# The prologue of a convolution and maxout kernel: x1's load moved up, work moved between ScalarE and GpSimd, a conv product made once instead of twice

## The chip, the cores and the metric

The kernel runs on one core of a Trainium2 chip. The metric is the device time of one execution in microseconds (us). The engines are named as in the profile: PE is TensorE's matmul, PEld its weight load, DVE is VectorE, ACT is ScalarE, POOL is GpSimd, SP is the engine that issues most of the DMA transfers. A q behind a name is the engine's sequencer.

## The reference

```
w = softmax(weight, axis=-1)                 # weight [8 heads, 7 taps], 1e-9 added to the sum
y[b, s, h, :] = sum over k of w[h, k] * x[b, s - 6 + k, h, :]    # zeros ahead of each sequence
h = maximum(maximum(y @ w1, y @ w2), y @ w3)                     # [tokens, 768]
out = h @ w_out                                                  # [tokens, 192]
```

x is 8 sequences of 4160 tokens by 192 channels in float32 (8 heads of 24 channels), w1, w2 and w3 are 192 x 768, w_out is 768 x 192. The output has 33280 tokens by 192 channels.

## The kernel before, in words

The 33280 tokens are cut into 65 blocks of 512. Every instruction is placed by hand: an engine executes its instructions in the order in which the program issues them, and waits only for semaphores on data and on buffers that it reuses.

The maxout is rewritten so that one of its three products becomes part of the output: with differences `wd` = w1 - w3 and w2 - w3 the hidden values are max(relu(y(w1 - w3)), y(w2 - w3)), and y(w3 w_out) is added to the output. `make_wd(n, j0, j1)` makes the differences (L312) for column tiles j0 to j1 of 128; wd[0] and wd[1] hold the first 128 channels of the two, wd[2] the last 64 of both (one in each half of the partitions), wd[3] a copy of half of wd[0] and wd[1] in the other half of the partitions (`cross_wd`, L323). `copy_w3` (L316) doubles the last 64 rows of w3 into the upper half of the partitions, which wd[2] needs. `cast_w3` (L320) casts w3 to float16 for `transpose_w3` (L338, L341), and `make_m` (L347, L349) multiplies w3 and w_out into `m16`.

The first four blocks ("dense", 0 to 3) are convolved in another way than the rest. `load_x(t)` (L167) brings 112-row windows of x; `cast_dense` (L216) casts them into two zeroed tiles xz, in which the heads' channels are kept apart, and `conv_dense` (L388) multiplies them with the banded matrix `band` of the taps, five windows (of 103 or 100 tokens) to a block. A matmul here fills 32 output partitions, so that four stand side by side in TensorE. The 192 channels are six slots of 32. Slots 0 to 3 go to PSUM tile D0, copied to yd[:, 0]; slots 4 and 5 go twice to PSUM tile D1, into both halves of the partitions, copied to yd[:, 2] (L393):

```
slots_ = ((0, 1, 2, 3), (4, 5, 4, 5))[n]
```

`cross` (L399) copies halves of yd[:, 0] across the partitions into yd[:, 1]. The hidden products of blocks 0 and 1 are made in pairs of column tiles by `l1_dense` (L541): "F" are the products over 128 channels, "H" the third products over the last 64; blocks 2 and 3 use `l1` (L517), with three products for each of two halves. `tops` and `top` (L500, L505) make relu and maximum on ACT and DVE. `first_hidden` (L613) and `first_rest` (L621, L626) make block 0's output, `st2` (L582) the others'; L589 and L590 add two PSUM halves of the output.

PSUM tiles come from three rotating pools: psp and psq have two buffers each, psw has four. pm0 and pm1 of `make_m` take the two buffers of psp, and the first product of block 2 (lp) takes the one that pm0 had. G, the conv's PSUM tiles of the later blocks, and po, the output's, share psw.

Later blocks (from 4 on) are loaded as 39-row windows into seven tiles xf, cast by POOL (L199), convolved in groups (L367), and turned by DMA transposes (L421); POOL copies the result across the halves (`double`, L430). Rows 32 to 63 of the tiles xf must be zero: `zero_x` does that, on ACT by a copy of zeros (L140) or on a named engine by a memset (L137).

The prologue's order on SP is x0, w3, w1 and w2 (128 rows, columns 0 to 255: `load_wa`, L229), the same columns of their last 64 rows (`load_wb`, L233), x1, and then the rest of the weights, w_out, x2, x3 and x4 to x6. Until the first conv can start, PE makes dummy products (L261).

Of the kernel before, what the change touches and what calls it, by code (L numbers as in the profile page):

```python
# [19 lines left out]
GRP = 24  # L20
BAND_W = 128 + PAD
NBLK = 512
CHK = 103
HALF = P // 2
# [4 lines left out]
def kernel(  # L29
# [12 lines left out]
    nc = tc.nc  # L42
# [3 lines left out]
    H, KWs = weight.shape  # L46
# [180 lines left out]
    def load_wa(f):  # L227
        for st, n, wsrc in ((w3s, 0, moe_w3), (ws, 0, moe_w1), (ws, 1, moe_w2)):
            nc.sync.dma_start(out=st[:, n, f], in_=wsrc[0:P, f])  # L229

    def load_wb(f):
        for st, lo, n, wsrc in ((w3s, 0, 1, moe_w3), (ws, 0, 2, moe_w1), (ws, HALF, 2, moe_w2)):
            nc.sync.dma_start(out=st[lo:lo + HALF, n, f], in_=wsrc[P:D, f])  # L233
# [6 lines left out]
    wos = const.tile([P, NJ, D], FP32)  # L240
    load_x(0)
    load_wa(slice(0, PW))
    load_wb(slice(0, PW))
    load_x(1)
    load_wa(slice(PW, 2 * PW))
    load_wb(slice(PW, DFF))
    load_wa(slice(2 * PW, DFF))
# [4 lines left out]
    make_identity(nc, ident[:])  # L252
    ident16 = const.tile([P, P], FP16)
    nc.gpsimd.tensor_copy(out=ident16[:], in_=ident[:])
    idle = const.tile([P, NBLK], FP16)
    nc.vector.memset(idle[:], 0.0)
    def keep_warm(widths, pool, tag):
# [24 lines left out]
    nc.vector.reciprocal(out=wrec[:], in_=wrec[:])  # L282
    zero_x(4)
    nc.vector.tensor_scalar_mul(out=line[0:NHEAD, 31:31 + KW], in0=wexp[:, 0:KW], scalar1=wrec[:])
    for v in range(2):
        nc.vector.memset(xz[1][v][:], 0.0)
    cast_dense(0, (nc.vector.tensor_copy, nc.vector.tensor_copy))
    CUT = 28
    for lo, hi, copy in ((0, CUT, nc.scalar.copy), (CUT, WIN, nc.vector.tensor_copy)):
        bps = psq.tile([32, hi - lo + 3, NHEAD], FP32, tag="q", name=f"band_{lo}")  # L290
        for c in range(lo, hi):
# [4 lines left out]
        for a in range(4):  # L296
            copy(out=band[32 * a:32 * a + 32, :, 32 * a + lo:32 * a + hi],
                 in_=bps[:, 0:hi - lo, :].rearrange("p c h -> p h c"))
    zero_x(5)
    keep_warm((NBLK,) * 3, psp, "p")  # L300


# [11 lines left out]
    def copy_w3(copy, j0, j1):  # L314
        f = slice(P * j0, P * j1)
        copy(out=w3s[HALF:P, 1, f], in_=w3s[0:HALF, 1, f])  # L316
# [56 lines left out]
            slots[t0] = ysp.tile([P, 2, nu, 2, D], FP16, tag="ys", name=f"ys_{t}")  # L373
        convs[t0] = G, heads[0]

    def conv_dense(t, copies, pools=((None, None),) * 2, order=(0, 1)):


        yd = dense[t] = ydp.tile([P, NC, NBLK], FP16, tag="yd", name=f"yd_{t}")
        for n in order:  # L380
            slots_ = ((0, 1, 2, 3), (4, 5, 4, 5))[n]
            pool, tag = pools[n]
            ps = (pool or psw).tile([P, NBLK], FP32, tag=tag or "w", name=f"D{n}_{t}")
            for (q, b, row_lo, rlen, lo, hi, cc) in chunks_of[t]:
                for v in range(2):
                    for g, s in enumerate(slots_):
                        h = (32 * s + 31 * v) // GRP
                        nc.tensor.matmul(  # L388
                            ps[32 * g:32 * g + 32, lo:hi],
                            lhsT=xz[t][v][0:rlen, q, 32 * s:32 * s + 32],  # L390
                            rhs=band[0:rlen, h, cc:cc + hi - lo],
                            start=(v == 0), stop=(v == 1), tile_position=(0, 32 * g))
            copies[n](out=yd[:, 2 * n, :], in_=ps[:])  # L393

    def cross(t, *copies):

# [294 lines left out]
    GP = nc.gpsimd.tensor_copy  # L691
    make_wd(0, 0, 2)
    make_wd(1, 0, 2)
    zero_x(6, 4, NR, nc.vector)
    conv_dense(0, (ACT, DVE))
    zero_x(6, 0, 4)
    for t in range(NDENSE, XBUF):
        load_x(t)
    copy_w3(DVE, 0, 2)
    make_wd(2, 0, 2)  # L700
    cast_dense(1, (GP, ACT), (1, 2, 0))
    l1_dense([(0, 0, PQ), (0, 1, PQ)], "F")
    cast_w3(0, 2)
    copy_w3(GP, 2, 6)
    make_wd(2, 2, 4, nc.gpsimd)
    for n in range(NC):
        make_wd(n, 4, 6, nc.gpsimd)
    cast_w3(2, 6)
    conv_dense(1, (DVE, ACT), order=(1, 0))
    make_wd(0, 2, 4)  # L710
    make_wd(1, 2, 4)
    cross_wd(0, GP)
    GP(out=wo[:], in_=wos[:])
    l1_dense([(0, 0, PQ), (0, 1, PQ)], "H")
    tops((0, 0), (0, 1))
    l1_dense([(1, 0, WW), (1, 1, WW)], "HF")
    tops((1, 0), (1, 1))
    l1_dense([(0, 2, PQ), (0, 3, PQ)], "FH")
    tops((0, 2), (0, 3))
    l1_dense([(1, 2, WW), (1, 3, WW)], "HF")  # L720
# [5 lines left out]
    tops((1, 4), (1, 5))  # L726
    transpose_w3((PQ[0], PQ[0], PQ[1]))
    cast_dense(3, (GP, GP))
    cross_wd(1, ACT)
    first_hidden(0)  # L730
    first_hidden(1)
    conv_dense(2, (ACT, DVE), (WW[0], PQ[1]))
    cast_x(4)
    cross(2, ACT, DVE)
    make_m(0)
# [26 lines left out]
    for t in range(2, NB):  # L762
        u = convs_at.get(t, NB)
        late = t > 2 and u < NB
        if t in (3, 4):
            double(t + 1)
        if t > 3:
            for v in range(casts.get(t - 1, 8) + 1, casts[t] + 1):
                cast_x(v)
        l1(t, 0)  # L770
        if t == 2:
            first_rest()
        elif t == 3:
            cast_x(8)
            nc.gpsimd.tensor_copy(out=m16[0:HALF, 2, :], in_=m16[HALF:P, 0, :])
            nc.gpsimd.tensor_copy(out=m16[HALF:P, 2, :], in_=m16[HALF:P, 1, :])
        if t > 3 and not late:
            op(lambda t=t: (store(t - 2, 0, 4, (nc.sync,)),
                            turn(t + 2, (2,)) if place(t + 2)[1:] in ((0, 4), (0, 5)) else None,
                            turn(t + 1, (4,)) if place(t + 1)[1:] == (0, 5) else None, load_on(t)))  # L780
        else:
            op(lambda t=t: store(t - 2, 0, 4, (nc.sync,)))
        cuts = ROOM if late else EVEN
        st2(t - 1, (cuts[0], cuts[0]))
        for j in range(1, NJ):
            l1(t, j)
            if late and j == 1:
                st2(t - 1, (cuts[0] + OWN + AHEAD, cuts[0] + OWN))
                meet()
                quad, second = u >= QUADS, u < QUADS or t == u - 3  # L790
                conv(u, WPWQ, range(4 * second, 4 * second + 4) if quad else range(NHEAD))
                for i in (0, 2):
                    evac(u, i)
                for i in (1, 3):
                    evac(u, i, nc.vector.tensor_copy)
                if second:
                    turn(u)
                load_on(t)
            if t == 2 and j == 1:
                meet()  # L800
                conv_dense(3, (ACT, DVE))
                zero_x(1, NQ, NR, nc.vector)
                cross(3, GP, GP)
                load_x(8)
                cast_x(6)
            elif t == 2 and j == 3:
                meet()
                conv(u, WW)
                evac(u, 0)
# [40 lines left out]
```

## Time and profile before

| what | value |
|---|---|
| median of 3 runs | 453.1 us (452.54 to 453.47) |
| profiled execution | 452.5 us, of which the profile's span is 450.7 us |
| PE, busy share of the span | 99% |
| DVE, ACT, POOL | 79%, 71%, 45% |
| granted TensorE clock | 1.0 |
| DMA, mean | 160 GB/s |
| first matmul of a dense conv | 6.22 us |
| first output store issued | 26.74 us |

All times inside a profile are counted from the start of its span. The profiled execution lies 0.6 us below the median of the runs. A row of the timeline gives start, duration, engine, source line, operation, the tiles out<-in, the shape, how often, and in brackets the idle time before it with what ended that. A merged row's duration is that of all its instructions together.

### The profile page before, as it was taken

The page shows a single profiled execution, that of the slowest core. Times are in us where ns is not written, and L with a number is a line of the kernel's source. Part 1 is how long each engine was busy: PE and PEld are TensorE (multiplying, and loading weights), DVE is VectorE, ACT ScalarE, POOL GpSimd, SP SyncE. Part 2 cuts the span into 40 slices and gives each one's busy share as a digit, 9 for nine tenths or more (in the row PEclk, how much of TensorE's full clock was granted, in tenths as well). Part 3 has the DMA queues.
Part 4 walks back from the last instruction along what each step waited for, and adds up shares of the span by engine and source line. Part 5 has one row for each costly group of instructions (what it writes and reads, how often), then busy time and mean ns, then how long its engine had stood idle before and what let it go on. Part 6 is the DMA issues. An engine that isn't in the chain of part 4 may idle for free.

```text
span 450.7 us, 18261 instructions
## 1 busy us (share of the span) xinstructions
PE 444.7 (99%) x7576; PEld 409.5 (91%) x7576; DVE 356.5 (79%) x610; ACT 320.3 (71%) x600; POOL 204.0 (45%) x234
## 2 busy tenths in 40 slices
PE   7999999999999999999999999999999999999997
PEld 4579999999999999999999999999999999999996
DVE  7778778878778787787887887887887887887775
ACT  7977677767677676776776777776776776776664
POOL 2874836556464524714724635526544545124000
PEclk9999999999999999999999999999999999999999
DMA  7978999495977759649559749769549566172123
GB/s 204 238 191 158 208 183 240 134 217 148 183 208 161 184 107 214 172 112 205 158 138 185 190 103 193 192 105 218 157 116 207 160 157 151 48 139 75 56 71 106
DMA packets 128242, 72.01 MB, mean 160 GB/s; under 512 B 52320, under 2 KB 127967, under 8 KB 128159
## 3 DMA queue, kind: packets, MB, share of 16 engines
q1 hardware_dynamic: 127999, 70.75, 68.8%
q8 instruction: 59, 0.97, 1.0%
q14 instruction: 24, 0.20, 0.2%
q10 hardware_dynamic: 160, 0.10, 0.1%
HBM read 33.28 MB, written 25.56 MB: 131 GB/s over the span
## 4 chain that ended last, share of the span: by engine, by line
PE 97%; DMA 1%; SPq 1%; issue 0%; DVE 0%; POOL 0%; POOLq 0%
PE po L582 36%; PE lq L517 32%; PE lp L517 22%; PE G L367 3%; PE lw L541 1%; DMA xf<-in_x_dram 1%; PE D L388 1%; PE lp L541 1%; PE po L613 0%; PE po L640 0%; SPq L233 0%; SPq L229 0%; PE pm L347 0%; PE lq L541 0%; SPq L167 0%; PE pt L338 0%
## 5 line engine op out<-in xcount | busy, mean ns | idle before, releaser
L582 PE MATMUL po<-wo,h 64*128 64x192 f16 x3024 | 331.7, 243 | 0.0
L505 DVE TENSOR_TENSOR h<-r,lq 128x512 f16<-128x512 f16 x384 | 263.0, 686 | 84.3 <-ACT r L500 74.3
L500 ACT ACTIVATE r<-lp 128x512 f16<-128x512 f32 x384 | 229.0, 597 | 113.4 <-PE lp L517 103.0
L517 PE MATMUL lp<-yp,wd 64*128 64x512 f16 x1098 | 295.6, 376 | 0.0
L517 PE MATMUL lq<-yp,wd 64*128 64x512 f16 x1098 | 295.5, 376 | 0.0
L582 PEld LDWEIGHTS <-h 64*128 64x128 f16 x3024 | 242.6, 94 | 5.5 <-issue 4.1
L517 PEld LDWEIGHTS <-wd 64*128 64x128 f16 x2268 | 181.6, 94 | 14.9 <-issue 0.2
L199 POOL CAST x<-xf 103x768 f16<-103x768 f32 x122 | 97.2, 825 | 112.4 <-DMA xf<-in_x_dram 108.9
L582 PE MATMUL po<-m,yp 64*128 64x192 f16 x720 | 140.3, 243 | 0.0
L430 POOL COPY yp<-yp 64x1536 f16<-64x1536 f16 (+1 forms) x70 | 90.9, 1298 | 87.3 <-DMA yp<-ys 62.3
L590 DVE TENSOR_TENSOR o<-a,po 128x384 f32<-128x384 f32 x126 | 69.0, 548 | 0.0
L582 PEld LDWEIGHTS <-yp 64*128 64x128 f16 x720 | 66.3, 94 | 0.1
L589 ACT COPY a<-po 128x384 f32<-128x384 f32 x126 | 59.5, 472 | 0.0
L407 ACT CAST ys<-G 128x480 f16<-128x480 f32 (+1 forms) x53 | 25.4, 530 | 9.5 <-PE G L367 9.5
L407 DVE CAST ys<-G 128x480 f16<-128x480 f32 (+1 forms) x53 | 30.2, 610 | 0.0
L367 PE MATMUL G<-x,band 39*32 39x240 f16 (+3 forms) x1024 | 16.5, 242 | 0.0
L367 PEld LDWEIGHTS <-band 39*32 39x32 f16 x1024 | 10.2, 91 | 4.6 <-issue 4.1
L517 PE MATMUL lq<-yd,wd 64*128 64x512 f16 x36 | 9.7, 376 | 0.0
L517 PE MATMUL lp<-yd,wd 64*128 64x512 f16 x36 | 9.7, 376 | 0.0
L541 PEld LDWEIGHTS <-wd 128*128 128x128 f16 (+1 forms) x48 | 3.1, 96 | 6.0 <-issue 2.8
L216 POOL CAST xz<-xf 112x160 f16<-112x160 f32 (+2 forms) x15 | 4.3, 330 | 7.9 <-DMA xf<-in_x_dram 7.8
L388 PEld LDWEIGHTS <-xz 112*32 112x32 f16 x320 | 3.9, 96 | 2.7 <-POOL xz L216 1.1
(79 smaller groups left out, 98.1 us busy)
## 6 DMA issues: line engine op xcount, KB each, us to landing
xf<-in_x_dram SPq DMA_DIRECT2D x113, 234.0 KB
out_dram<-o SPq DMA_DIRECT2D x62, 384.0 KB
wall<-in_moe_w_dram SPq DMA_DIRECT2D x12, 128.0 KB
xf<-in_x_dram SPq DMA_DIRECT2D x7, 204.8 KB
xf<-in_x_dram SPq DMA_DIRECT2D x3, 420.0 KB
yp<-ys SPq DMA_TRANSPOSE x70
out_dram<-o SPq DMA_DIRECT2D x5, 192.0 KB
wos<-in_moe_w_out_dram SPq DMA_DIRECT2D x1, 576.0 KB
```

Source lines behind the costliest of these rows:

```text
L199: nc.gpsimd.tensor_copy(out=x16s[t0][0:K, :, :, u, r, :].rearrange("p h j c -> p j h c"), in_=xf[0:K, 4 * r:4 * r + 4, :].rearrange("p j ( ...
L367: nc.tensor.matmul(G[2 * (k // per) + i][TOK * j:TOK * (j + 1), k % per, :], lhsT=band[row, h, HALF * i + LAP:HALF * i + KR], rhs=x16s[t0] ...
L388: nc.tensor.matmul(ps[32 * g:32 * g + 32, lo:hi], lhsT=xz[t][v][0:rlen, q, 32 * s:32 * s + 32], rhs=band[0:rlen, h, cc:cc + hi - lo], star ...
L407: copy(out=slots[t][:, i % 2, :, :, GRP * h0:GRP * (h0 + per)].rearrange("p u r (h c) -> p h (u r) c", c=GRP), in_=G[i][:].rearrange("p h ...
L430: nc.gpsimd.tensor_copy(out=yp[HALF * i:HALF * (i + 1), 1, :, :, :, :].rearrange("p i u k n -> p (i u k n)"), in_=yp[HALF * (1 - i):HALF * ...
L500: nc.scalar.activation(out=r[:], in_=ps[0][:], func=AF.Relu)
L505: nc.vector.tensor_max(out=hs[t][:, j, :], in0=r[:], in1=q[:])
L517: nc.tensor.matmul(ps[i][:], lhsT=w_of(i, c, j), rhs=y_all(t, i, c), start=(n == 0), stop=(n == NC - 1))
L541: nc.tensor.matmul(open_ps[t, j, i][:], lhsT=a, rhs=b, start=(t, j, i) not in begun, stop=(t, j, i) in begun)
L582: nc.tensor.matmul(ps[b0, i][:, s % 2, :], lhsT=a, rhs=b, start=first, stop=last)
L589: nc.scalar.copy(out=a[:], in_=ps[s - 1, 0][:])
L590: nc.vector.tensor_add(out=outs[t][:, s - 1:s + 1, :], in0=a[:], in1=ps[s - 1, 1][:])
```

## The change

1. x1 is loaded after the 128-row slices of the first weight columns and ahead of their 64-row slices.
2. The zeroing of xz[1] moves from DVE to POOL, that of x5 from ACT to POOL, that of x6 from DVE and ACT to POOL.
3. The cut of the band copies moves from 28 to 25, so that ACT copies 25 columns and DVE 13.
4. `conv_dense` makes slots 4 and 5 once, not twice. Windows 0 to 2 go to the lower half of the partitions and windows 3 and 4 to the upper one; windows 0 and 3, and 1 and 4, are issued together, so that four matmuls still stand side by side. It has 60 matmuls instead of 80. The PSUM tile then has half of yd[:, 2] in each half of the partitions, and each half is copied twice, to its own partitions and to the other ones; in block 1 the second copy is made by POOL from the first (`dup`).
5. Block 1's conv stands ahead of block 0's third products ("H"), and block 1's first pair is made in the order F, H.
6. Casts, copies and differences of the weights change engines and order: x1's casts go to DVE and POOL (from POOL and ACT), `copy_w3` goes to ACT, POOL, ACT, `cast_w3` is one instruction, and `cross_wd(0)` moves from POOL to ACT, ahead of `cross_wd(1)`.

```diff
     load_x(0)
     load_wa(slice(0, PW))
+    load_x(1)
     load_wb(slice(0, PW))
-    load_x(1)
...
+    for v in range(2):
+        nc.gpsimd.memset(xz[1][v][:], 0.0)
...
-    for v in range(2):
-        nc.vector.memset(xz[1][v][:], 0.0)
...
-    CUT = 28
+    CUT = 25
...
-    zero_x(5)
+    zero_x(5, eng=nc.gpsimd)
...
-    def conv_dense(t, copies, pools=((None, None),) * 2, order=(0, 1)):
+    def conv_dense(t, copies, pools=((None, None),) * 2, order=(0, 1), dup=None):
...
+        ch = chunks_of[t]
+        FAR = (NQ + 1) // 2
         for n in order:
-            slots_ = ((0, 1, 2, 3), (4, 5, 4, 5))[n]
+            if n == 0:
+                units = [[(c, 0, (0, 1, 2, 3))] for c in ch]
+            else:
+                units = [[(c, 2 * (c[0] // FAR), (4, 5)) for c in ch[k::FAR]] for k in range(FAR)]
...
-            copies[n](out=yd[:, 2 * n, :], in_=ps[:])
+            if n == 0:
+                copies[0](out=yd[:, 0, :], in_=ps[:])
+            else:
+                far = ch[FAR][4]
+                for i, (lo, hi) in enumerate(((0, far), (far, NBLK))):
+                    own, other = (slice(HALF * k, HALF * (k + 1)) for k in (i, 1 - i))
+                    copies[1 + i](out=yd[own, 2, lo:hi], in_=ps[own, lo:hi])
+                    if dup is None:
+                        copies[1 + i](out=yd[other, 2, lo:hi], in_=ps[own, lo:hi])
+                    else:
+                        dup(out=yd[other, 2, lo:hi], in_=yd[own, 2, lo:hi])
...
-    zero_x(6, 4, NR, nc.vector)
-    conv_dense(0, (ACT, DVE))
-    zero_x(6, 0, 4)
-    for t in range(NDENSE, XBUF):
-        load_x(t)
-    copy_w3(DVE, 0, 2)
-    make_wd(2, 0, 2)
-    cast_dense(1, (GP, ACT), (1, 2, 0))
-    l1_dense([(0, 0, PQ), (0, 1, PQ)], "F")
-    cast_w3(0, 2)
-    copy_w3(GP, 2, 6)
-    make_wd(2, 2, 4, nc.gpsimd)
-    for n in range(NC):
-        make_wd(n, 4, 6, nc.gpsimd)
-    cast_w3(2, 6)
-    conv_dense(1, (DVE, ACT), order=(1, 0))
-    make_wd(0, 2, 4)
-    make_wd(1, 2, 4)
-    cross_wd(0, GP)
-    GP(out=wo[:], in_=wos[:])
-    l1_dense([(0, 0, PQ), (0, 1, PQ)], "H")
-    tops((0, 0), (0, 1))
-    l1_dense([(1, 0, WW), (1, 1, WW)], "HF")
-    tops((1, 0), (1, 1))
+    conv_dense(0, (ACT, ACT, DVE))
+    cast_dense(1, (DVE, GP), (1, 2, 0))
+    l1_dense([(0, 0, PQ), (0, 1, PQ)], "F")
+    copy_w3(ACT, 0, 2)
+    make_wd(2, 0, 2)
+    zero_x(6, eng=nc.gpsimd)
+    conv_dense(1, (ACT, DVE, DVE), dup=GP)
+    make_wd(0, 2, 4)
+    make_wd(1, 2, 4, nc.gpsimd)
+    copy_w3(GP, 2, 4)
+    make_wd(2, 2, 4, nc.gpsimd)
+    l1_dense([(0, 0, PQ), (0, 1, PQ)], "H")
+    tops((0, 0), (0, 1))
+    l1_dense([(1, 0, WW), (1, 1, WW)], "FH")
+    tops((1, 0), (1, 1))
+    copy_w3(ACT, 4, 6)
+    for n in range(NC):
+        make_wd(n, 4, 6, nc.gpsimd)
+    cast_w3(0, 6)
+    GP(out=wo[:], in_=wos[:])
+    for t in range(NDENSE, XBUF):
+        load_x(t)
...
     cast_dense(3, (GP, GP))
+    cross_wd(0, ACT)
     cross_wd(1, ACT)
...
-    conv_dense(2, (ACT, DVE), (WW[0], PQ[1]))
+    conv_dense(2, (ACT, DVE, ACT), (WW[0], PQ[1]))
...
-                conv_dense(3, (ACT, DVE))
+                conv_dense(3, (ACT, DVE, ACT))
```

More of the change, by code (lines that the diff above doesn't have):

```diff
@@ L382, in conv_dense @@
             pool, tag = pools[n]
             ps = (pool or psw).tile([P, NBLK], FP32, tag=tag or "w", name=f"D{n}_{t}")
-            for (q, b, row_lo, rlen, lo, hi, cc) in chunks_of[t]:
+            for unit in units:
                 for v in range(2):
[L386 to L392, printed above, removed]
@@ L393, in conv_dense @@
-            copies[n](out=yd[:, 2 * n, :], in_=ps[:])
+                    for (q, b, row_lo, rlen, lo, hi, cc), g0, slots_ in unit:
+                        for g, s in enumerate(slots_, g0):
+                            h = (32 * s + 31 * v) // GRP
+                            nc.tensor.matmul(
+                                ps[32 * g:32 * g + 32, lo:hi],
+                                lhsT=xz[t][v][0:rlen, q, 32 * s:32 * s + 32],
+                                rhs=band[0:rlen, h, cc:cc + hi - lo],
+                                start=(v == 0), stop=(v == 1), tile_position=(0, 32 * g))
```

## The prediction

> **What bounds the kernel now.** I read the page's busy shares first, then the chain that ended last, then the timeline of the first 31 us, with the waits inside it.
>
> ```profile
> PE 444.7 (99%) x7576; PEld 409.5 (91%) x7576; DVE 356.5 (79%) x610; ACT 320.3 (71%) x600; POOL 204.0 (45%) x234
> ...
> PE 97%; DMA 1%; SPq 1%; issue 0%; DVE 0%; POOL 0%; POOLq 0%
> ```
>
> TensorE (PE) is busy for 99% of the span and carries 97% of the chain. In the built programs the instructions from block 3's conv onward stand in the same order on every engine, so later blocks run at PE's pace in both versions: whatever PE is late or early at about 31 us is the change in the total. Only the prologue is left to work out. These are its rows (start us, duration us, engine, line, tiles, idle before and what ended it).
>
> ```profile
> 6.11 1.47 ACT L140 CAST xf<-idle 32x1536 f32<-32x1536 f16 x1
> 7.60 0.59 ACT L393 CAST yd<-D 128x512 f16<-128x512 f32 x1
> 8.24 0.59 PE L541 MATMUL lp<-yd,wd 128*128 128x512 f16 x2 [0.91 <-ACT yd L393]
> 9.87 1.30 PE L388 MATMUL D<-band,xz 112*32 112x103 f16 x80 [0.61 <-POOL xz L216]
> 12.56 0.61 POOL L316 COPY wall<-wall 64x512 f32<-64x512 f32 x1 [1.66 <-DMA wall<-in_moe_w_dram]
> 13.38 2.96 POOL L312 TENSOR_TENSOR wd<-wall 128x256 f16<-128x256 f32 x4 [0.20 <-DMA wall<-in_moe_w_dram]
> 14.15 0.55 PEld L541 LDWEIGHTS <-wd 64*128 64x128 f16 x8 [0.47 <-POOL wd L312]
> ...
> 19.80 1.60 ACT L341 CAST w3t<-pt 128x512 f16<-128x512 f32 x3
> 21.42 0.83 ACT L323 COPY wd<-wd 64x768 f16<-64x768 f16 x1
> 22.32 0.59 ACT L393 CAST yd<-D 128x512 f16<-128x512 f32 x1
> 22.65 1.16 PE L347 MATMUL pm<-wo,w3t 128*128 128x192 f16 x12
> 22.93 0.62 ACT L399 COPY yd<-yd 64x512 f16<-64x512 f16 x1
> 23.46 0.71 ACT L349 CAST m<-pm 128x192 f16<-128x192 f32 x2
> 23.81 0.37 PE L517 MATMUL lp<-yd,wd 64*128 64x512 f16 x1
> ```
>
> Three places matter. Up to 9.87 PE waits for zeroing on ACT and for x1. At 14.15 it waits for the second pair of wd columns, which waits for the weights to land. From 19.80 to 23.76 ACT runs without a pause, and PE's first product of block 2 (23.81) follows ACT's first m copy (ended 23.76), because it writes the PSUM buffer that pm0 has just left. PE itself could have started at about 23.74: ACT already sets that point, by little.
>
> **Stage one, to 14.1 us: a gain that does not last.** zero_x(5) leaves ACT (1.47 us), so yd of block 0 is copied when its matmuls are done (about 6.8, not 7.60) and the first product starts near 7.4 instead of 8.24. The casts of x0 on DVE lose the 0.97 us of memsets ahead of them, but wait for x0, whose last DMA update is at 4.15; CUT 25 gives DVE 24 more elements in each of four band copies, about 0.1 us. Block 0's conv starts 0.1 to 0.2 earlier. x1 (0.59 us to issue, 430 KB) passes three weight loads (327 KB) on SP's queue; they issue 0.6 us later. It landed at 9.36; less 327 KB at the rate of this stretch (1.15 MB from 4.15 to 9.36, 0.22 MB/us) it is at about 7.9. Its casts on DVE stand behind block 0's two second-slot copies; those wait, in the built program, for ACT's two copies of the same PSUM tile (7.4 to 8.25), and end near 9.05. ACT's first copy of w3 now waits for a load that is 1.5 us later (about 8.6 to 9.0); what stands behind it, block 1's yd copy, is not wanted before 10.2. So block 1's conv starts near 9.5, not 9.87; block 0's third products near 10.3, not 11.10; the first products of block 0's tiles 2 and 3 near 12.3, not 13.15.
>
> Their third products then need wd[2] of those columns. Before: 13.38 plus 0.72 on POOL, and PE at 14.15. After: the same bytes are ahead of these weights, so they land when they did (w2's slice has its last DMA update at 12.05, the last one of the three small loads at 13.21). POOL does wd[1] (0.72, from 12.15), the copy of w3 (half the 0.61 of the row, plus overhead: about 0.37) and wd[2] (0.72): 14.05, PE at 14.1. The 0.85 us are gone. Bounds: earlier landings leave POOL's own chain, whose start is then block 1's copies on POOL (end 11.7): 0.35 gained; if the order makes the weights 0.6 late (a last update trails the other fifteen by up to 1.1 here), 0.6 lost. I take 0, as bytes and order behind x1 are unchanged.
>
> The memsets on POOL cost nothing while they lie in its idle 1.7 to 9.5: by its rows of 1, 128 and 192 elements (103, 204, 248 ns), 0.8 us for each xz[1] tile, 1.3 for each zero_x. The loads of x4 to x6 keep their place on SP. The w3 casts in one piece end near 17.5, wanted at 18.80; wo ends near 18.95 (its DMA's last update 17.75), wanted at 19.55.
>
> **Stage two, to 23.8 us: the ACT chain.** cross_wd(0) moves from POOL, where its 0.91 us ended at 18.29 with nobody waiting, into ACT's queue behind the w3t copies: 0.83 us by the equal row at 21.42. Block 2's second slot gives ACT two copies of 64x203 that DVE had: by m's copies of 192 columns (0.31) 0.33 each. Nothing leaves. The chain is then 21.42 + 0.83 + 0.02 + 0.83 = 23.10; yd 0.59 to 23.71; two copies to 24.41; cross 0.62 to 25.05; m 0.31 to 25.38; PE at 25.43. That is **1.62 us later** than 23.81. PE's conv is shorter (16 rounds of four matmuls instead of 20, at 46 ns, which is the row's 1.10 us less the last one's 0.21 over its rounds: 0.18 us), which here only lengthens its wait.
>
> **Stage three, block 3's conv, to 31 us.**
>
> ```profile
> 26.34 1.10 PE L388 MATMUL D<-band,xz 112*32 112x103 f16 x80
> ...
> 27.04 0.59 ACT L393 CAST yd<-D 128x512 f16<-128x512 f32 x1
> 27.07 0.69 DVE L505 TENSOR_TENSOR h<-r,lq 128x512 f16<-128x512 f16 x1 [0.39 <-ACT r L500]
> ...
> 27.67 0.68 DVE L393 CAST yd<-D 128x512 f16<-128x512 f32 x1
> ...
> 28.64 0.60 ACT L500 ACTIVATE r<-lp 128x512 f16<-128x512 f32 x1 [1.02 <-PE lq L517]
> ```
>
> ACT had 1.02 us idle before 28.64. Now its second-slot copies wait for DVE's two (the built program holds that semaphore), and DVE's stand behind h. Shifted by 1.62, h ends at 29.38; two DVE copies of 64x309 (0.47 each, between the rows of 80 elements at 0.23 and 512 at 0.69) end near 30.3; ACT's two end near 31.0, so r starts there: 28.64 + 2.37. Behind it on ACT is the copy a (0.47), then h and the sum o (0.55) on DVE, which frees the PSUM tile for PE's second output products: 30.48 before, about 32.85 after. Sum: 1.62 - 0.18 (conv) + 0.93 (this wait) = **2.4 us slower**.
>
> Made against the profiled execution, that is 450.7 + 2.4 = 453.1 of span and 452.5 + 2.4 = 454.9 of time; that execution lies 0.6 below the median, so I forecast 453.1 + 2.4 = 455.5 us. A measurement of this kernel can tell about 0.2%, 0.9 us.
>
> **A rule beside stage three.** The Trainium skill, page "PSUM — Partial Sum Buffer", section "PSUM bank collisions raise a hardware error", has two engines excluded from one bank only within the same 32 partitions, with guarding by the whole bank as the simple form. The two halves here lie in different partitions, so by that rule ACT need not wait for DVE and the total would be 1.62 - 0.18 = 1.44; the built program guards anyway, and no trace shows it without.
>
> **Rivals.**
>
> *POOL's memset holds up DVE's casts.* zero_x(6) runs on POOL from about 8.85 to 10.15, and DVE wants to cast x1 at 9.05. For it: at 23.49 a DVE copy of 64x512 took 0.58 us and ended 0.15 after the POOL cast beside it, while DVE's copy at 8.89, POOL idle, took 0.29 for 256 elements of twice the size. Casts at 10.2 would put block 1's copies on POOL and wd[2] 0.7 us later (0.4 of slack is eaten first): PE at 14.85, total 2.4 + 0.7, 456.2 us. Against it: no memset was beside a DVE cast, and if x1 lands 0.3 us later the casts come first. Chance 0.22. The Trainium skill, "SBUF — State Buffer", "Who interferes with whom", makes it a rule: a DVE copy or cast that uses both its ports and a GpSimd instruction exclude each other for a whole instruction.
>
> *Only the first stall.* ACT's wait in stage three hides in its idle 1.02 us: 1.44 us, 454.5. It decides if ACT's last copy ends before about 30.1, against 31.0 by the sum. Chance 0.12.
>
> *Early gain kept, one stall.* The weights do not gate: 1.44 - 0.85, 453.7. Against it stands the wait of 0.47 us at 14.15, which ended with the landing. Chance 0.08.
>
> *Faster.* The gain of 0.85 at 7.4 us survives, and ACT's chain does not set PE's start at block 2, so that both shorter convs count: 453.1 - 0.85 - 0.36 = 451.9. It needs ACT's m copy done by 23.6 where the sum has 25.38; only w3t copies 1.8 us earlier would do it. Chance 0.06.
>
> **How the numbers follow.** The forecast has 0.46, and 0.06 is left for a third stall above 456.8 (x loads or block 4's transposes 2 us late; POOL had them doubled at 37.76, wanted at 40.09). Low end: only the first stall, weights 0.35 early and 0.4 of spread between runs, 453.8. High end: the memset rival and weights 0.6 late, 456.8. Inside lie 0.46 + 0.22 + 0.12 = 0.80. Faster by over 0.2% is the fourth rival, 0.06; within 0.2% the third, 0.08; slower the rest, 0.86.
>
> **What would show it.** Right: PE's first product at 7.4 but its third products of tiles 2 and 3 at 14.1 again; two L323 copies in a row on ACT; PE idle for over 1.5 us before block 2, ended by ACT's m copy; ACT idle for about 1 us on DVE before its copies of block 3. Wrong: block 2's first product before 24.5, or a shift at 31 us that differs from the one at the end.

## The result

The changed kernel takes 457.7 us at the median of five runs (456.9 to 459.0), against 452.5 us for the kernel before in the same session: a ratio of 1.0102, 95% interval 1.0074 to 1.013. The forecast was 455.5 with a range of 453.8 to 456.8. The direction was right, the size was not: the change costs about twice what the sum said. One run of all that follow, of 461.18 us, was in a slower state of the chip: the ratios leave it out, the medians do not.

The page of the profiled execution (458.18 us, span 456.4), its busy shares, the granted clock by slices and the chain of waits by engine:

```profile
PE 447.1 (98%) x7496; PEld 409.6 (90%) x7496; DVE 357.2 (78%) x612; ACT 320.8 (70%) x604; POOL 208.9 (46%) x239
...
PEclk9989999999999999999999999999999999999999
...
PE 92%; POOL 2%; DMA 2%; ACT 1%; SPq 1%; DVE 1%; issue 1%; POOLq 0%; DVEq 0%; ACTq 0%
```

PE's share of the chain fell from 97% to 92%; POOL now has 2% of it. The third slice of the clock (23 to 34 us) shows an 8, where before it was 9 throughout. The timeline of the prologue:

```profile
3.40 1.37 POOL L137 MEMSET xf<- 32x1536 f32 x1
3.46 1.33 DVE L286 TENSOR_SCALAR line<-wexp,wrec 8x7 f16<-8x7 f32 x1
...
4.84 1.20 PE L293 MATMUL band<-ident,line 128*32 128x32 f16 x38 [1.03 <-DVE line L286]
...
7.37 1.56 PE L394 MATMUL D<-band,xz 112*32 112x103 f16 x60
...
8.47 0.59 ACT L400 CAST yd<-D 128x512 f16<-128x512 f32 x1 [1.40 <-PE D L394]
...
9.11 1.01 PE L557 MATMUL lp<-yd,wd 128*128 128x512 f16 x2 [0.18 <-ACT yd L400]
...
9.88 0.37 DVE L405 CAST yd<-D 64x203 f16<-64x203 f32 x1 [1.93 <-ACT yd L407]
...
10.56 0.53 DVE L216 CAST xz<-xf 112x160 f16<-112x160 f32 x3
...
11.24 0.91 PE L394 MATMUL D<-band,xz 112*32 112x103 f16 x60 [0.48 <-DVE xz L216]
...
12.76 1.01 POOL L409 COPY yd<-yd 64x309 f16<-64x309 f16 x2 [2.10 <-DVE yd L405]
...
13.86 0.72 POOL L312 TENSOR_TENSOR wd<-wall 128x256 f16<-128x256 f32 x1
...
15.90 0.39 PE L557 MATMUL lp<-yd,wd 64*128 64x512 f16 x1 [0.49 <-POOL wd L312]
...
23.16 1.69 ACT L323 COPY wd<-wd 64x768 f16<-64x768 f16 x2
...
25.48 0.32 ACT L405 CAST yd<-D 64x203 f16<-64x203 f32 x1
...
27.18 0.37 PE L533 MATMUL lp<-yd,wd 64*128 64x512 f16 x1 [1.88 <-ACT m L349]
...
33.66 0.32 ACT L405 CAST yd<-D 64x203 f16<-64x203 f32 x1 [1.10 <-DVE yd L407]
```

The first two rows show the first trouble: the memset is new on POOL, the second instruction was there before. That 8x7 instruction that writes `line` took 0.22 us before and takes 1.33 now: it ends 0.02 us after the memset beside it. PE waits 1.03 us for it, and block 0's conv starts at 7.37 instead of 6.22. Block 1's conv (11.24 instead of 9.87) and the third products of tiles 2 and 3 (15.90 instead of 14.16) are late behind it, though not by this alone.

The same rows show a second thing. Block 0's conv takes 1.56 us, block 1's 60 matmuls of the same shapes 0.91, and the two first products take 1.01 us where they took 0.59 before: PE is still at its slow pace at 9 us. The clock column gives 1.00 for this stretch all the same, so ahead of about 10 us here it is the rows' durations that tell the pace.

The lower rows are those of the prediction: two cross copies in a row on ACT, PE idle until ACT's copy of m, ACT waiting for DVE in block 3.

The view by stretches of time of the same execution gives, after the busy times, the granted clock (PEclk):

```profile
core 0: us, PE busy (x) PEld busy (x) DVE busy (x) ACT busy (x) POOL busy (x), PEclk, DMA share, GB/s
26.00:28.00 2.00, 0.82 (x6) 0.22 (x5) 1.08 (x2) 1.93 (x5) 1.28 (x2) 0.87 0.06 17
28.00:30.00 2.00, 2.00 (x18) 1.32 (x18) 0.98 (x2) 1.03 (x3) 0.00 (x0) 0.50 0.37 96
30.00:32.00 2.00, 2.00 (x72) 1.19 (x67) 0.20 (x1) 0.71 (x3) 0.00 (x0) 0.78 0.48 116
```

Right behind PE's idle 1.88 us the clock is at one half for about 3.4 us, in which PE does the same products more slowly. Nothing in the prediction had this, nor the slow pace at the start.

How far PE is behind the kernel before, by the starts of the same work, in the profiled execution and in a second one (next section):

| place | predicted | profiled | second |
|---|---|---|---|
| block 2's conv (21.61 before) | 0 | +1.68 | +2.29 |
| block 2's first product (23.81) | +1.62 | +3.37 | +3.98 |
| block 3's conv (26.34) | +1.62 | +4.93 | +3.98 |
| products behind it | +1.44 | +4.74 | +3.80 |
| behind ACT's wait for DVE, at about 31 us | +2.37 | +5.70 | +4.74 |
| end | +2.37 | +5.7 | +5.9 |

The steps of stages two and three are as predicted: 1.69 (1.62), -0.19 (-0.18), 0.96 (0.93). Two are not: 1.7 to 2.3 us in stage one instead of nothing, and 1.56 us (4.93 - 3.37) at half clock in one execution of the two.

### The profile page after: what moved, and what is told of

Its sections match the earlier page's. It is cut to its first block, busy times and chain, and to the rows that moved or that the text cites. A ratio compares the mean times of both kernels' runs of the same rounds, so it can differ in the third digit from the quotient of the medians.

```text
span 456.4 us, 18111 instructions
## 1 busy us (share of the span) xinstructions
PE 447.1 (98%) x7496; PEld 409.6 (90%) x7496; DVE 357.2 (78%) x612; ACT 320.8 (70%) x604; POOL 208.9 (46%) x239
## 4 chain that ended last, share of the span: by engine, by line
PE 92%; POOL 2%; DMA 2%; ACT 1%; SPq 1%; DVE 1%; issue 1%; POOLq 0%; DVEq 0%; ACTq 0%
PE po L598 36%; PE lq L533 31%; PE lp L533 21%; PE G L367 3%; DMA xf<-in_x_dram 1%; POOL wd L312 1%; SPq L229 1%; POOL xz L216 1%; DMA wall<-in_moe_w_dram 0%; PE po L656 0%; ACT wd L323 0%; POOL wo L729 0%; ACT r L516 0%; SPq L233 0%; POOL w3h L320 0%
## 5 line engine op out<-in xcount | busy, mean ns | idle before, releaser
L533 PEld LDWEIGHTS <-wd 64*128 64x128 f16 x2268 | 182.0, 94 | 17.1 <-issue 2.3
L367 PEld LDWEIGHTS <-band 39*32 39x32 f16 x1024 | 10.2, 91 | 4.6 <-issue 4.1
L598 PE MATMUL po<-m,yd 64*128 64x192 f16 x36 | 6.2, 254 | 0.9 <-DVE o L606 0.6
```

What stands on the lines that cost most here:

```text
L367: nc.tensor.matmul(G[2 * (k // per) + i][TOK * j:TOK * (j + 1), k % per, :], lhsT=band[row, h, HALF * i + LAP:HALF * i + KR], rhs=x16s[t0] ...
L533: nc.tensor.matmul(ps[i][:], lhsT=w_of(i, c, j), rhs=y_all(t, i, c), start=(n == 0), stop=(n == NC - 1))
L598: nc.tensor.matmul(ps[b0, i][:, s % 2, :], lhsT=a, rhs=b, start=first, stop=last)
```

## The experiments

They ran on four chips, whose medians of the kernel before were 452.9 to 453.6 us, so medians of different rows can differ by up to 0.8 us for that alone. The ratio is to the runs of the kernel before in the same call; the other columns are from each kernel's one profiled execution. "Conv 1" is the start of block 1's conv, "third" that of the third products of tiles 2 and 3, "2 to p" the time from block 2's conv to its first product, "2 to 3" that from block 2's conv to block 3's.

| kernel | median us | ratio, 95% | line | conv 1 | third | 2 to p | 2 to 3 |
|---|---|---|---|---|---|---|---|
| before (columns of its first profile) | 453.24 | | 0.22 | 9.87 | 14.16 | 2.20 | 4.73 |
| changed, again | 457.79 | 1.008 to 1.0115 | 1.33 | 11.85 | 16.51 | 3.89 | 6.42 |
| zeroing as before | 456.77 | 1.0056 to 1.0099 | 0.22 | 10.51 | 15.59 | 3.89 | 7.95 |
| block 5's zeroing as before | 458.6 | 1.0075 to 1.0123 | 0.22 | 11.47 | 17.84 | 3.88 | 7.28 |
| PE's idle time filled | 458.63 | 1.0099 to 1.0138 | 1.33 | 11.97 | 17.39 | 3.77 | 6.29 |
| block 3's conv as before | 457.33 | 1.0073 to 1.0137 | 1.33 | 11.42 | 16.08 | 3.88 | 6.40 |
| cross copies on DVE | 457.19 | 1.0077 to 1.011 | 1.33 | 12.03 | 16.69 | 3.72 | 6.24 |
| part copies on DVE | 456.77 | 1.0047 to 1.0102 | 1.33 | 11.87 | 16.54 | 3.08 | 5.60 |
| both on DVE | 456.28 | 1.0042 to 1.0081 | 1.34 | 11.56 | 16.23 | 2.20 | 5.70 |
| three costs undone | 455.9 | 1.0032 to 1.0088 | 0.22 | 10.12 | 14.80 | 2.23 | 4.89 |
| and all convs as before | 453.93 | 1.0003 to 1.0024 | 0.22 | 9.42 | 13.92 | 2.20 | 4.72 |
| before, two edits | 453.55 | 0.9997 to 1.0025 | 0.22 | 8.89 | 13.26 | 2.20 | 4.72 |
| before, three edits | 453.33 | 0.9995 to 1.0021 | 0.22 | 9.04 | 13.45 | 2.51 | 5.03 |

### The base: the changed kernel again

> The changed kernel once more, unaltered, as the base for its variants on this chip and for the spread between executions. Theory A (three parts of different kind: GpSimd's memsets shutting out VectorE, ScalarE's longer chain, and a half clock after TensorE's 1.88 us idle before block 2, that comes in some executions): time 457.5 to 458.7; line's instruction again 1.2 to 1.4 us; the casts of x1 on VectorE between 0.5 and 1.8 us, by how far they overlap the memset of block 6's pad rows, whose start follows x1's landing; the clock below 1.0 in about 2 runs of 5. Rival: the delays of the first profile were of that one execution, and line's instruction is back near 0.22 us here.

Theory A held. `line` took 1.33 us again. One of the six runs had a mean clock of 0.996, where 2 of 5 were expected. Two rows of its view by stretches show that the half clock does not come in every execution, though PE was idle for the same 1.88 us before block 2:

```profile
26.00:28.00 2.00, 0.21 (x2) 0.11 (x3) 1.40 (x3) 1.89 (x7) 1.89 (x3) 1.00 0.11 27
28.00:30.00 2.00, 2.00 (x28) 1.18 (x26) 0.69 (x2) 1.73 (x3) 0.00 (x0) 1.00 0.14 36
```

What was saved there was lost elsewhere: x1 came 0.65 us later (POOL's first cast of it at 9.04, not 8.39), so the second memset (9.94 to 11.31) lay on the casts of x1 on DVE, which took 1.15 us instead of 0.53.

### The zeroing

All of it back:

```diff
-    for v in range(2):
-        nc.gpsimd.memset(xz[1][v][:], 0.0)
...
-    zero_x(5, eng=nc.gpsimd)
+    zero_x(5)
...
+    zero_x(6, 4, NR, nc.vector)
     conv_dense(0, (ACT, ACT, DVE))
+    zero_x(6, 0, 4)
...
-    zero_x(6, eng=nc.gpsimd)
```

> The changed kernel with all zeroing where it was before (block 1's tiles by VectorE, block 5's and 6's pad rows by ScalarE and VectorE); everything else changed. Theory A (GpSimd's fp32 zeroing keeps VectorE's SBUF-to-SBUF instructions waiting until it ends): the 8x7 instruction that writes line is back at 0.22 us instead of 1.33, block 0's conv starts at 6.2 to 6.4 us instead of 7.37, block 1's conv near 10.3 instead of 11.24, the third products of tiles 2 and 3 at 14.5 to 15.2 instead of 15.90, and the end is 0.7 to 1.4 us earlier: 456.3 to 457.0. Rival B (the late third products come from the weights' or x1's later landing, not from the zeroing): line gets its 0.22 us back, but the third products of tiles 2 and 3 still start at 15.7 to 15.9 and the time stays at 457.3 to 458.2.

`line` is at 0.22 us and block 0's conv at 6.28, but block 1's conv starts only at 10.51, because in this execution x1 came late and DVE's casts of it, beside POOL's, took 0.89 us instead of 0.53:

```profile
6.28 0.94 PE L394 MATMUL D<-band,xz 112*32 112x103 f16 x60
...
9.60 1.30 POOL L216 CAST xz<-xf 112x160 f16<-112x160 f32 x3 [7.93 <-DMA xf<-in_x_dram]
...
10.51 0.23 PE L394 MATMUL D<-band,xz 112*32 112x103 f16 x4 [1.36 <-DVE xz L216]
...
15.59 0.39 PE L557 MATMUL lp<-yd,wd 64*128 64x512 f16 x1 [0.50 <-POOL wd L312]
```

The median is 1.0 us lower than that of the changed kernel, as A has it, though the intervals overlap; the third products are nearly as late as B has them, which speaks for a second cause. This run alone does not tell them apart. Only block 5's memset back on ACT:

```diff
-    zero_x(5, eng=nc.gpsimd)
+    zero_x(5)
```

> The changed kernel with block 5's pad rows zeroed by ScalarE as before; block 1's tiles and block 6's pad rows stay on GpSimd. Theory A (each of GpSimd's memsets shuts out VectorE's SBUF-to-SBUF work): line takes 0.22 us, block 0's conv starts at 6.1 to 6.3 us, its copies are done about 0.9 us earlier, and VectorE's casts of x1 then run into the memset of block 6's pad rows (9.29 to 10.66): the first of these casts starts at about 9.7 and ends only with the memset, so block 1's conv comes at 10.9 to 11.1, hardly earlier than 11.24, and the end gains 0 to 0.4 us: 457.2 to 457.7. Rival (only the first memset matters): block 1's conv moves with block 0's to about 10.3, and the end gains 0.9 us or more: 456.3 to 456.9.

Theory A's step is there in plain sight; these are the timeline's rows:

```profile
9.53 1.79 DVE L216 CAST xz<-xf 112x160 f16<-112x160 f32 x3
9.68 1.50 POOL L137 MEMSET xf<- 32x1536 f32 x1
...
11.47 1.56 PE L394 MATMUL D<-band,xz 112*32 112x103 f16 x60 [2.32 <-DVE xz L216]
```

The first two casts take 0.23 and 0.19 us; the third, 1.53 us, ends 0.14 us after the memset. The early gain is gone, and with PE's idle 2.32 us comes a clock of 0.50 for 6.8 us (10.2 to 17.1), which neither theory had: four of the six runs had a mean clock of 0.996 or less, and the median of 458.6 is not better at all, where A had 457.2 to 457.7.

Block 1's conv here gives the pace at a clock of 0.50: 60 matmuls in 1.56 us. That is what block 0's conv took in the changed kernel. It took 1.51 to 1.56 us in all seven executions of this study in which `line` took 1.33 us and PE waited 1.03 us for it, and 0.94, 1.16 and 1.32 in the three with 60 matmuls and `line` at 0.22. So the late `line` goes together with a longer slow pace at the start.

In all these traces only DVE's casts from SBUF to SBUF, and the scalar multiplication that writes `line`, are held. Its copies from PSUM beside the memset take 0.37 us as always (9.88 in the changed kernel), its own memsets of xz beside POOL's 0.97 as before, its two reductions of the taps beside POOL's memsets of xz 0.13 and 0.15 as before, and ACT's copy of w3 beside the memset 0.40. A maximum of two SBUF tiles is not held either. It took 0.44 us before, and these are the rows of the kernel with all convs as before, further down:

```profile
16.31 1.37 POOL L137 MEMSET xf<- 32x1536 f32 x1
...
17.04 0.43 DVE L521 TENSOR_TENSOR h<-r,q 128x512 f16<-128x512 f16 x1
```

### The clock

```diff
     make_m(0)
     make_m(1)
+    keep_warm((NBLK,) * 6, psw, "w")
```

> The changed kernel with six more matmuls of zeros (256 columns wide tile of 512, no use made of them) on TensorE behind the sums for the block diagonal weights, where it sat idle for 1.88 us before block 2's first product. Nothing that ScalarE or VectorE does moves, so block 2's first product stays within 0.2 us of 27.18. Theory A (that idle time is what takes the clock to half for 3.4 us, in some executions): the granted clock stays at 1.0 in the profile and in every one of the runs, block 3's conv starts near 29.7 instead of 31.27, and the median falls to the changed kernel's runs at clock 1.0: 456.7 to 457.4. Rival (the clock falls for another reason): some runs still show 0.996, and the median stays at 457.7.

PE's own timeline, and the clock by stretches:

```profile
11.97 1.49 PE L394 MATMUL D<-band,xz 112*32 112x103 f16 x60 [1.85 <-DVE xz L216]
29.07 0.37 PE L533 MATMUL lp<-yd,wd 64*128 64x512 f16 x1 [0.47 <-ACT m L349]
```

```profile
13.00:16.00 3.00, 3.00 (x30) 0.92 (x20) 2.40 (x5) 1.66 (x3) 1.75 (x4) 0.58 0.88 260
...
28.00:30.00 2.00, 1.53 (x11) 0.59 (x10) 1.08 (x2) 1.90 (x6) 0.57 (x1) 1.00 0.00 0
```

With the idle time before block 2 filled, the clock stays at 1.0 there; 1.85 us of idle time before block 1's conv, for the late casts of x1, now brought the half clock instead. The expectation that no run would show it missed, and so did the one on the time: 458.6 us, though five of six runs had a clock of 1.0. Why those were no faster is open. The unaltered kernel also had five of six runs at 1.0, so this run does not prove that filling the idle time is what kept the clock. Over the twelve profiles and the first one of the changed kernel, once PE had come up to its full pace, of seven idle times from 1.85 to 2.32 us five went with a half clock, and of those up to 1.71 us none.

### Block 3's conv as before

```diff
-                conv_dense(3, (ACT, DVE, ACT))
+                conv_dense(3, (ACT, DVE), twice=True)
```

(`twice` makes both halves of slots 4 and 5 as the kernel before did.)

> The changed kernel with block 3's dense conv made as before (all three chunks from TensorE: two whole copies, one by ScalarE and one by VectorE, instead of one conv and four part copies). Theory A (the prediction's stage three: ScalarE's part copies of the third chunk wait for VectorE's, and the second products wait for them, 0.96 us less 0.18 for the shorter conv): ScalarE's 1.10 us wait at 33.66 is gone, the products of block 3's first tiles come 0.7 to 0.9 us earlier from there on, and the time is 456.8 to 457.1. Rival (the wait is hidden by TensorE's queue of products): within 0.2 us of 457.7.

The wait at ACT is gone: PE is +3.53 us behind the kernel before at block 3's conv and still +3.53 at 40 us, where the changed kernel goes on losing 0.96 - 0.19. That is the 0.77 us of stage three. The median, 457.3, lies 0.5 under the changed kernel's, between what the two theories had; the intervals overlap, since three of its six runs had a clock of 0.996 or less.

### The chain on ACT

Three kernels. The cross copies on DVE:

```diff
-    cross_wd(0, ACT)
-    cross_wd(1, ACT)
+    cross_wd(0, DVE)
+    cross_wd(1, DVE)
```

> The changed kernel with both cross copies of the w1 - w3 and w2 - w3 columns (64x768) on VectorE instead of ScalarE; VectorE sat idle for 1.95 us ahead of its first copy of block 2's conv. Theory A (ScalarE's chain of 1.69 us more is what holds up block 2's first product): ScalarE's copy of block 2's conv follows the conv at once, the first product comes 2.2 to 2.5 us behind the start of block 2's conv instead of 3.89, TensorE's idle of 1.88 us before it is under 0.5, the clock stays at 1.0 from there on, and the time falls by 1.4 to 2.2 us: 455.6 to 456.4 against 457.8. Rival C (VectorE's two copies from SBUF to SBUF are shut out by GpSimd's twelve casts of x2 and x3, which follow one another from about 20.5 to 24.1 us): they take over 2 us, VectorE's copies of the conv come after them, and the first product is no earlier than in the changed kernel: 457.5 to 459.0.

```profile
23.13 0.88 DVE L323 COPY wd<-wd 64x768 f16<-64x768 f16 x2
...
24.78 0.58 ACT L400 CAST yd<-D 128x512 f16<-128x512 f32 x1 [0.85 <-PE D L394]
...
25.55 0.47 DVE L407 CAST yd<-D 64x309 f16<-64x309 f32 x1
...
26.11 0.32 ACT L405 CAST yd<-D 64x203 f16<-64x203 f32 x1 [0.74 <-PE pm L347]
...
27.80 0.37 PE L533 MATMUL lp<-yd,wd 64*128 64x512 f16 x1 [1.71 <-ACT m L349]
```

Theory A misses, and of rival C only the late first product is there. The copies take 0.88 us beside POOL's casts, so they are not shut out; ACT's chain is 1.69 us shorter and its copy of block 2's conv waits for PE alone; but the first product gains 0.17 us. ACT's part copies now wait 0.74 us. The profile puts that down to PE's pm, but in the built program these copies wait for DVE's second part copy, the row above, which ends at 26.02; the distance of 0.09 us to it is the one that ACT's copy at 33.66 in the changed kernel has to DVE's (33.57). The four part copies on DVE:

```diff
-    conv_dense(2, (ACT, DVE, ACT), (WW[0], PQ[1]))
+    conv_dense(2, (ACT, DVE, DVE), (WW[0], PQ[1]))
```

> The changed kernel with all four part copies of the third chunk of block 2's conv on VectorE (in the change, VectorE has two and ScalarE two). Theory A (on ScalarE's chain, each instruction counts, as the prediction added it up: two cross copies 0.83 each and two part copies 0.32): ScalarE's chain is 0.66 us shorter, block 2's first product comes 3.2 us behind the start of block 2's conv instead of 3.89, and the time falls by 0.5 to 0.8 us: 456.9 to 457.3 against 457.8. Rival D (the first product waits for VectorE's part copies as well): four copies in a row on VectorE end 1.6 us after the conv, which is 2.6 us behind its start, so they are not later than ScalarE's chain, and the time is the same as by theory A; only if block 2's first product stays at 3.7 or more behind the conv is the chain on ScalarE not what sets it.

3.08 us from conv to product instead of 3.89, 0.81 gained, and block 3's conv 0.82 earlier: theory A, a little more than it had. The median of 456.8 is lower than the changed kernel's too, though the intervals overlap. Both edits together:

> The changed kernel with both cross copies and all four part copies of block 2's third chunk on VectorE. With the cross copies alone on VectorE the first product came 3.72 us behind the conv's start (3.89 in the changed kernel), because ScalarE's part copies then waited for VectorE's. Theory A+ (either of the two, the cross copies or the wait for VectorE's part copies, is enough to hold ScalarE; only both together set it free): ScalarE has one copy of the conv, one cross copy and the copy of m, the first product comes 2.3 to 2.6 us behind the conv's start, and the time falls by 1.2 to 1.6 us to 456.2 to 456.6. Rival: VectorE's row is now the longer one, or PE waits elsewhere, and the gain is under 0.8 us.

```profile
25.82 0.37 PE L533 MATMUL lp<-yd,wd 64*128 64x512 f16 x1 [0.19 <-ACT m L349]
26.36 0.37 PE L533 MATMUL lp<-yd,wd 64*128 64x512 f16 x1 [0.15 <-DVE yd L407]
27.25 0.37 PE L533 MATMUL lq<-yd,wd 64*128 64x512 f16 x1 [0.29 <-DVE yd L415]
```

The first product comes 2.20 us after the conv, as before the change. Then PE waits for DVE's row in small pieces, and block 3's conv is again 5.70 us behind block 2's, 0.97 more than before and no better than the 5.60 with the part copies alone. So both theories have a part: the median of 456.3 and the 2.20 us are A+'s, together the two edits set ACT free, but DVE takes its place.

### The order, and repairs

Zeroing as in the first diff of this section, both convs of blocks 2 and 3 with `twice=True`, and `cross_wd(0)` on POOL at its place:

> The changed kernel with the zeroing, the dense convs of blocks 2 and 3 and the engine of cross_wd(0) as before. What is left of the change: x1 loaded earlier, block 1's conv ahead of block 0's third products, blocks 0 and 1's convs with the third chunk once, CUT 25. Theory A (zeroing, ScalarE's chain and block 3's part copies are the whole cost, and the idle of TensorE before block 2 with its half clock goes with them): block 2's first product 2.2 to 2.5 us behind block 2's conv, no half clock, and the time is that of before within 0.2%: 452.4 to 454.2 against 453.3. Rival B (the new order costs as well, since GpSimd's two part copies of block 1's third chunk now stand ahead of its weight differences): the third products of tiles 2 and 3 stay at 15.2 to 15.6 instead of 14.16 us, and the time is 454.3 to 454.9.

Then blocks 0 and 1 with `twice=True` as well, with block 6's memset on POOL behind its weight differences:

> As the kernel before this one (zeroing as before, but block 6's pad rows on GpSimd behind its weight differences; cross_wd(0) on GpSimd), with all four dense convs as before. Left of the change: x1 loaded earlier, block 1's conv ahead of block 0's third products, CUT 25, and the division of copies and casts among engines. Theory B (part copies on GpSimd ahead of the weight differences are what makes the third products of tiles 2 and 3 late): without them GpSimd starts the differences when the weights have landed (about 12 to 13 us), these products start at 14.0 to 14.4, and the time is 452.4 to 453.5, 1 us or more under the kernel with part copies. Theory A (the order costs nothing): no difference beyond 0.3 us between the two.

The timeline of the first of the two, then of the second:

```profile
11.74 0.93 POOL L409 COPY yd<-yd 64x309 f16<-64x309 f16 x2 [2.26 <-DVE yd L405]
...
12.76 0.72 POOL L312 TENSOR_TENSOR wd<-wall 128x256 f16<-128x256 f32 x1
...
14.80 0.39 PE L557 MATMUL lp<-yd,wd 64*128 64x512 f16 x1 [0.49 <-POOL wd L312]
```

```profile
11.88 0.72 POOL L312 TENSOR_TENSOR wd<-wall 128x256 f16<-128x256 f32 x1 [2.41 <-DMA wall<-in_moe_w_dram]
...
13.92 0.39 PE L557 MATMUL lp<-yd,wd 64*128 64x512 f16 x1 [0.32 <-POOL wd L312]
```

In the profile with three costs undone the third products come at 14.80, 1.10 before the changed kernel's, and the profiled time is 454.3. Its median is 455.9, with four of eleven runs at a clock of 0.996. In the profiled execution PE still waits 0.96 us for block 1's conv, though x1 came early; that it waits longer in those four is not shown. Without POOL's part copies the differences wait for the weights alone, the third products are at 13.92, and the median is 453.9, just above the kernel before. So theory B is right that POOL's part copies cost as well, 0.88 us at that place (12.76 against 11.88).

Both medians lie above what was expected. The gain of 0.88 us does not last in the two profiles: with all convs as before, PE waits for POOL's cast of w_out, which now stands behind block 6's memset, and block 2's first product comes at 24.62, against 24.42 with three costs undone. What the medians differ by goes with the clock: seven runs of the first kernel had a clock of 1.0, with a median of 454.4, and all twelve of the second had one of 0.999 or more.

Last, two edits on the kernel before, and then a third one:

```diff
     load_wa(slice(0, PW))
+    load_x(1)
     load_wb(slice(0, PW))
-    load_x(1)
...
-    zero_x(5)
+    zero_x(5, eng=nc.gpsimd)
```

> The kernel before with two edits alone: x1 loaded between the 128-row and the 64-row weights, and block 5's pad rows zeroed by GpSimd, where nothing stands ahead of that memset (about 1.7 to 3.1 us, beside memsets and reductions of VectorE only). Theory A (only VectorE's copies, casts and arithmetic from SBUF to SBUF are shut out by a GpSimd memset): line's instruction stays at 0.22 us, the first product starts at 7.3 to 7.5 us instead of 8.24. By the prediction's stage one the gain dies at the weights' landing: third products of tiles 2 and 3 at 13.9 to 14.2, block 2's first product 23.5 to 23.9, time 452.6 to 453.8 against 453.3. Rival (the early gain is kept): 452.3 to 452.6 and block 2's first product near 23.0.

```diff
-    cross_wd(0, GP)
     GP(out=wo[:], in_=wos[:])
+    cross_wd(0, GP)
```

> The kernel with x1 loaded earlier and block 5's pad rows zeroed by GpSimd (two edits on the kernel before), and a third: GpSimd casts w_out before it copies the cross columns, not after. In the run with two edits TensorE waited 0.59 us at 19.79 for that cast, which stood behind the 0.82 us cross copy. Theory A (the early gain is lost only there): the output products start at 19.1 to 19.3 us, block 2's first product at 23.4 to 23.7 instead of 24.06 (23.81 before), and the time is 0.2 to 0.4 us under the kernel before: 452.8 to 453.1 against 453.24. Rival (the next gate is as late: GpSimd's casts of x2 or ScalarE's chain of 1.6 us from the transposes on): block 2's first product stays at 23.8 to 24.1, no difference.

The rows are of the kernel with two edits:

```profile
3.46 0.22 DVE L284 TENSOR_SCALAR line<-wexp,wrec 8x7 f16<-8x7 f32 x1
...
13.26 0.39 PE L541 MATMUL lp<-yd,wd 64*128 64x512 f16 x1
...
19.79 2.14 PE L613 MATMUL po<-wo,h 128*128 128x192 f16 x24 [0.59 <-POOL wo L713]
```

The same memset on the same engine costs nothing when it does not lie beside such an instruction of DVE. The first product starts at 7.58 and the third ones 0.90 us earlier than before, and the gain dies, later than expected: PE waits for POOL's cast of w_out, and block 2's first product is at 24.06 (23.81 before). With the cast ahead of the cross copy the output products start at 19.36, but block 2's first product is at 23.95, as the rival had it. No version beat the kernel before by more than a measurement tells.

## Why the prediction was wrong, step by step

**Stage one failed.** The step is "the memsets on POOL cost nothing while they lie in its idle 1.7 to 9.5". It asked only whether POOL was free, not what DVE does at that time. The prediction knew the mechanism, as a rival with a chance of 0.22, but looked for it only at the memset of x6 and the casts of x1; the memset of x5 meets `line` at 3.46, which every matmul of the band waits for. The Trainium skill, "SBUF — State Buffer", "Who interferes with whom", lists tensor_scalar with copy and cast among the operations that can take both ports, and says that whoever is second waits for a whole instruction; the trace agrees with 1.33 us for an instruction of 0.22.

The 0.4 us of slack counted there was not left either. x1 was to land at 7.9; POOL's first cast of it started between 8.39 and 9.60 us in the thirteen profiles with x1 loaded earlier. Block 0's copies follow each other, ACT's three and then DVE's two, from 8.47 to 10.64, where the sum had them ended by 9.05. Block 1's conv came at 11.24 and not at 9.5, 1.74 us late. Of this about 1.3 are block 0's conv, which started at 7.37 and not at about 6.1. Another 0.4 are PE's slow pace: ACT's first copy starts 1.10 us behind the start of block 0's conv, and 0.70 behind that of block 1's (11.94). The sum took PE's pace in block 0's conv for granted; that the wait for `line` is what kept it slow is argued from the ten executions compared above.

The third products came at 15.90 and not at 14.1, 1.80 late. Of the 1.98 us between 15.90 and the 13.92 of the last repair, 0.88 go with the part copies on POOL, which the sum had ended by 11.7, ahead of the weights, and which ended at 13.77. The other 1.10 go with the zeroing in two executions in which x1 came early (8.39 and 8.63); with x1 at 9.60 undoing the zeroing gave only 0.31 (15.59).

"The gain does not last" was right as far as it went, with another reason: in the kernel with two edits it passes the weights and dies at w_out's cast.

**Stage two was right, in size and in the path.** 1.69 against 1.62, with ACT running without a pause from 21.53 to block 2's first product. What the sum did not show is how close another chain lay. DVE's part copies, for which ACT's wait, ended at 25.23, and ACT's own copy ahead of them at 25.46. Taking 1.69 us off ACT gained 0.17, taking the part copies off ACT 0.81, both 1.69.

**Stage three was right**: ACT idle for 1.10 us on DVE, +0.96 (0.93) and -0.19 (-0.18), and with block 3's conv as before both are gone. The trace shows again that ACT's part copies start after DVE's, though the two read different partitions.

**The half clock was missing altogether.** The prediction forecast PE idle for over 1.5 us before block 2 and took this time as all that it costs. In the profiled execution 1.56 us were added. As that does not come in every execution, the rest must explain the runs at a clock of 1.0, and it does: 452.5 us of the kernel before and the 4.74 us that the second execution had lost at 31 us make 457.2, beside 456.9, 457.3 and 457.7 us for the changed kernel's three such runs. The second execution itself, at 458.35 us, lost another 1.15 us between 60 and 80 us (last section).

Of the signs that the prediction named, two cross copies in a row, PE's idle time and ACT's wait were there; the first product at 7.4 (9.11) and the third ones at 14.1 were not. Of its signs of being wrong, one came in the second execution, 4.74 us behind at 31 us and 5.9 at the end.

## What to carry to other kernels

Before work is moved to GpSimd because it is idle there, list which casts and scalar operations VectorE does from SBUF to SBUF in that time and who waits for them; the shortest instruction on the way to the first matmul can cost the whole length of a memset. A sum along one engine's queue tells the time, but not what a shorter queue would bring: take the instructions away in thought and ask which other chain is then the latest. And price an idle time of TensorE of about 2 us as possibly more than itself, and one of 1 us too while TensorE is still coming up to its pace.

## What the runs showed of the hardware

A GpSimd memset, which reads nothing, held VectorE's casts from SBUF to SBUF until it ended (three that took 0.53 us without it took up to 1.79), and so an 8x7 scalar multiplication (1.33 us instead of 0.22). VectorE's memsets, its copies from PSUM, two small reductions and a maximum of two SBUF tiles, and ScalarE's copies, ran on beside it. Fp16 copies of VectorE beside a row of short GpSimd casts were not shut out: 0.88 us for two.

The granted clock went to one half with idle times of 1.85 us or more in five cases of seven, for about 3.4 us in four of them and for 6.8 in one. With PE idle for 1.03 us before it had come up to its full pace, it was still at the slow pace at 7.4 us (60 matmuls in 1.51 to 1.56 us) in all seven such executions. The Trainium skill, "TensorE: Matmul & The Clock Gate", Part 1, has a free-running window of about 3.4 us, which agrees with the length (3.41 us in the profiled execution) and with its coming only in some executions; that it takes an idle window of about that length differs from the 1.85 us seen here.

In seven of the twelve profiles of the experiments, and not in the first two, PE falls back once more by 0.4 to 1.2 us between 60 and 80 us. The profile puts this down to "issue" in five of them and to ACT in one; from the second execution of the changed kernel:

```profile
66.08 0.37 PE L533 MATMUL lp<-yp,wd 64*128 64x512 f16 x1 [0.88 <-issue]
```

What it is stays open, and it limits what one execution can tell to about 1 us.
